# Giving the tile scheduler the order of every engine in an adaLN attention and MLP kernel, and splitting the modulation by PSUM bank

## The chip, the core and the metric

The kernel runs on one core of a Trainium2 chip. A core has TensorE (PE, with its weight loads shown as PEld), VectorE (DVE), ScalarE (ACT), GpSimd (POOL) and SyncE (SP, which here only issues DMAs). The metric is device time in microseconds (us) of one execution, the median over runs; the reading below is of one profiled execution.

## What is computed

One transformer layer on x of 2048 x 448 in bf16, with six modulation vectors made from c:

```
x = A_x
mod = (silu(c) @ w_mod).reshape(1, 6, 1, 448)
sa, ca, ga, sb, cb, gb = mod[:, 0], ..., mod[:, 5]
h = layernorm(x) * (1 + ca) + sa
x = x + ga * A_ref(h, A_wqkv, A_wo)
h = layernorm(x) * (1 + cb) + sb
x = x + gb * B_ref(h, B_w1, B_w2)
```

`A_ref` is attention with 16 heads of 28 columns, in which position s sees the 8 positions s, s-2, ..., s-14 (those below zero masked). `B_ref` is silu(h @ w1) @ w2 with 1792 hidden columns.

## The kernel before

Since attention reaches back in steps of 2, even and odd positions don't meet. They are two sequences ("parities") of 1024 positions, each of 8 tiles of 128 rows (u = 0 to 7 and 8 to 15) and of 9 attention blocks of up to 114 queries. A parity is worked in three groups, of 4, 3 and 2 blocks, so there are six groups, k = 0 to 5.

The steps of one group, with their lines:

- **LN1** (`stats` L174 to L177, normalize L185 or L449, `transposes` L195, `modulate` L204 on ACT and L206 on DVE): statistics of each tile on DVE (`BN_STATS`, `BN_AGGR`), 1/sqrt on POOL as an add and a pow, the normalised tile `xn` on DVE, four PE transposes for each tile into `ps_t`, and the modulation into `h1T`. For LN1 the four 112-row pieces k = 0 to 3 of `ps_t` are divided between DVE and ACT. `ps_t` takes two PSUM banks, k = 0, 1 in one and k = 2, 3 in the other.
- **project** (`qk_unit` L235, L237; `v_unit` L243, L245): q and k of a column range in four PSUM tiles of 8 matmuls each, cast to `qk` by ACT or DVE; v by blocks.
- **logits** (L265, `Exp` on ACT L267, mask on DVE L302), **attention times v** (`av` L330, reciprocal L332, scale L335; `tr` L343, L344), **output projection** with the residual (L350, L351).
- **LN2** as LN1, into `h2T`, all on DVE; **MLP** (f1: L395 and `Silu` on ACT L396; f2: L411, L415 and the store L416).

`late_mod` makes the other four modulation vectors: 32 matmuls L215 into `ps_m`, two gates of 4 matmuls L223 into `ps_g`, a copy of each gate on ACT (L224), and `wo` times its gate on DVE (L480). `gate_w2` multiplies `w2` by its gate on DVE, in two halves (L483). `check_sums` (L428 to L434) reduces the softmax sums to one flag, which every engine loads into a register; if the flag is positive the whole layer runs again in a safe form.

**What sets the order.** The Python code emits "units" in a written order; `weave` mixes a main list with a filler list by estimated costs. All of it stands under `with tc.manual_schedule():`, so each engine executes its instructions exactly in the order in which the code emits them. Within an engine an instruction that waits holds all those behind it. In that order the LN1 units of tiles 8 to 11 and 12 to 15 come at the end of the list of k = 0, woven with the output projections of that group, and the first projection of parity 1 comes in the filler of k = 1. `late_mod` is the last filler of the logits of k = 0; both halves of `gate_w2` are the last filler of the logits of k = 1. PSUM has two pools: `big`, three tiles of two banks (`ps_t`, `ps_qk`, `ps_v`, `ps_l`, `ps_h`), and `one`, two tiles of one bank (`ps_m`, `ps_g`, `ps_o`, `ps_ot`, `ps_wo`, `ps_y`, `ps_f`).

Of the kernel before, what the change touches and what calls it, by code (L numbers as in the profile page):

```python
# [23 lines left out]
HALO = 16  # L24
# [42 lines left out]
def layer(ctx, tc, io, safe):  # L67
# [13 lines left out]
    def ct(shape, name, dt=BF16):  # L81
        return const.tile(shape, dt, name=name)
# [32 lines left out]
    h1T = [ct([KP, KT, CW], f"h1T{p}") for p in range(2)]  # L115
# [51 lines left out]
    def stats(us):  # L167

        n = len(us)
        st = small.tile([128, 4, 6], F32, name="st")  # L170
        mv = small.tile([128, 4, 2], F32, name="mv", bufs=4)
        rs = small.tile([128, 4], F32, name="rs", bufs=4)
        for j, u in enumerate(us):
            V.bn_stats(out=st[:, j, :], in_=x_all[:, u, :])  # L174
            V.bn_aggr(out=mv[:, j, :], in_=st[:, j, :])  # L175
        G.tensor_tensor(out=rs[:, 0:n], in0=mv[:, 0:n, 1], in1=epsb[:, 0:n], op=ALU.add)  # L176
        G.tensor_tensor(out=rs[:, 0:n], in0=rs[:, 0:n], in1=negh[:, 0:n], op=ALU.pow)  # L177
        return mv, rs
# [10 lines left out]
    def transposes(ts, ps=None, j0=0):  # L189
        if ps is None:  # L190
            ps = big.tile([128, KT, 512], BF16, name="ps_t", tag="big")
        for j, t in enumerate(ts):
            c0 = 128 * (j0 + j)
            for k in range(KT):
                T.transpose(ps[:, k, c0:c0 + 128], t[:, KP * k:KP * k + 128], ident[:])  # L195
        return ps

    def modulate(ps, p0, n, dst, c0, which, act=()):

        for k in range(KT):  # L200
            o, i = dst[:, k, c0:c0 + n], ps[0:KP, k, p0:p0 + n]
            scale, shift = modc[:, 2 * which + 1, k:k + 1], modc[:, 2 * which, k:k + 1]
            if k in act:
                S.activation(out=o, in_=i, func=ACTF.Identity, scale=scale, bias=shift)  # L204
            else:
                V.tensor_scalar(out=o, in0=i, scalar1=scale, scalar2=shift, op0=ALU.mult, op1=ALU.add)  # L206
# [214 lines left out]
    def check_sums():  # L421

        n = 2 * NB * H
        ok = small.tile([128, n], F32, name="ok", bufs=1)
        cnt = small.tile([128, 1], F32, name="cnt", bufs=1)
        flag = small.tile([1, 1], I32, name="flag", bufs=1)
        rcf = rc[:].rearrange("p b h -> p (b h)")
        V.tensor_scalar(out=ok[:], in0=rcf, scalar1=LO, scalar2=None, op0=ALU.is_ge)  # L428
        V.scalar_tensor_tensor(out=ok[:], in0=rcf, scalar=HI, in1=ok[:], op0=ALU.is_le, op1=ALU.mult)
        V.tensor_reduce(out=cnt[:], in_=ok[:], axis=AX.X, op=ALU.add)  # L430
        ps = one.tile([128, 512], F32, name="ps_f", tag="one")
        T.matmul(ps[0:1, 0:1], lhsT=cnt[:], rhs=onesf[:], start=True, stop=True)
        V.tensor_scalar(out=flag[:], in0=ps[0:1, 0:1], scalar1=-1.0, scalar2=float(128 * n), op0=ALU.mult, op1=ALU.add)  # L433
        return nc.values_load(flag[:], min_val=0, max_val=128 * n)  # L434


    def ln1_units(us):
        held = {}

        def st():  # L440
            held["s"] = stats(us)

        def norm():
            mv, rs = held["s"]
            held["x"] = []
            for j, u in enumerate(us):
                t = xn[xc[0] % NX]
                xc[0] += 1
                V.tensor_scalar(out=t[:, 0:D], in0=x_all[:, u, :], scalar1=mv[:, j, 0:1], scalar2=rs[:, j:j + 1], op0=ALU.subtract, op1=ALU.mult)  # L449
                held["x"].append(t)  # L450

        def tr():
            ps = transposes(held["x"])
            modulate(ps, 0, 128 * len(us), h1T[us[0] // 8], HALO + 128 * (us[0] % 8), 0, act=(1, 3))
        return [(10.0, st), (10.0, norm), (900.0, tr)]

    st0 = stats([0, 1])
# [6 lines left out]
    ps0 = transposes(xa)  # L464
    xb = normalize([2, 3], *st1)
    mod_cols((0, 1), 0)
    ps1 = transposes(xb)
    modulate(ps0, 0, 256, h1T[0], HALO, 0, act=(1, 3))
    modulate(ps1, 0, 256, h1T[0], HALO + 256, 0, act=(1, 3))
    for kk in range(KT):  # L470
        V.tensor_copy(out=wp[:, kk, :, 0:DH], in_=wqkv[:, kk, 0:2 * D].rearrange("p (h d) -> p h d", d=DH))  # L471
    consts_late()
# [32 lines left out]
    if not safe:  # L505
        bad = check_sums()
# [6 lines left out]
@with_exitstack  # L513
def kernel(
    ctx: ExitStack,
    tc: tile.TileContext,
    A_x: bass.AP,
    A_wqkv: bass.AP,
    A_wo: bass.AP,
    B_x: bass.AP,  # L520
    B_w1: bass.AP,
    B_w2: bass.AP,
    c: bass.AP,
    w_mod: bass.AP,
    out: bass.AP,
):
    io = (A_x, A_wqkv, A_wo, B_w1, B_w2, c, w_mod, out)
    with ExitStack() as first:
        with tc.manual_schedule():
            bad = layer(first, tc, io, False)  # L530
    with tc.If(bad > 0):
        with ExitStack() as again:
            layer(again, tc, io, True)
# [30 lines left out]
```

## Time and profile before

| what | us |
|---|---|
| median of 3 runs (lowest, highest) | 246.09 (245.1, 246.82) |
| the profiled execution's own time | 246.31 |
| its span, first to last instruction | 244.5 |
| PE busy, and the five engines' next: DVE, ACT | 196.3, 125.3, 102.9 |
| PE busy in 57 to 81 us | 7.70 of 24.00 |
| PE busy in 99 to 219 us | 113.6 of 120.0 |

The profiled execution took 0.22 us more than the median. PE is the busiest engine, so the first thing to look for is where it has nothing to do. It stands idle in five places: while the first inputs load and LN1 of the first tiles is made (0 to 22 us), between 57 and 81 us, around 97 us, around 141 and 174 us, and briefly at 219 us.

### The profile page before, as it was taken

How to read it: one execution, taken by the hardware profiler on the slowest of the kernel's cores; microseconds unless marked ns; L12 is line 12 of the kernel's file. 1: busy time of each engine (PE TensorE's matmuls, PEld its weight loads, DVE VectorE, ACT ScalarE, POOL GpSimd, SP SyncE). 2: the span in 40 equal slices, each digit the busy share in tenths (PEclk: the TensorE clock that was granted, in tenths of full speed). 3: DMA queues.
4: the chain of work that ended last, by engine and by line, in shares of the span. 5: the costliest groups of instructions: out<-in, count | busy, mean ns of one | idle time of the engine just before them, and what ended most of it. 6: DMA issues, size and time to landing. Idle time of an engine off the chain costs nothing.

```text
span 244.5 us, 4117 instructions
## 1 busy us (share of the span) xinstructions
PE 196.3 (80%) x1739; PEld 118.7 (49%) x1739; DVE 125.3 (51%) x274; ACT 102.9 (42%) x133; POOL 16.8 (7%) x55
## 2 busy tenths in 40 slices
PE   0555979982522997899999959899599999989992
PEld 0413445661321544555665434786346555645760
DVE  4474406686683358557444164675357475554111
ACT  2032397701206157245543744624465373650330
POOL 3801000001030000010000100000100010010000
PEclk9998999998555699999999988999889999999999
DMA  6999995000000000000100001000000001000101
GB/s 166 249 227 230 235 213 165 4 3 0 0 0 0 3 0 1 3 0 20 39 0 3 0 5 35 20 3 0 3 19 21 0 0 40 19 0 23 38 5 44
DMA packets 9073, 11.22 MB, mean 46 GB/s; under 512 B 473, under 2 KB 8153, under 8 KB 9049
## 3 DMA queue, kind: packets, MB, share of 16 engines
q1 hardware_dynamic: 9040, 10.90, 18.7%
q8 instruction: 15, 0.25, 0.5%
q14 instruction: 10, 0.07, 0.1%
q10 hardware_dynamic: 8, 0.00, 0.0%
HBM read 9.06 MB, written 1.84 MB: 45 GB/s over the span
## 4 chain that ended last, share of the span: by engine, by line
PE 67%; DVE 15%; ACT 8%; DMA 3%; issue 3%; POOL 1%; SPq 0%; ACTq 0%
PE ps_h L395 18%; PE ps_y L411 17%; PE ps_qk L235 10%; PE ps_v L243 5%; PE ps_wo L350 5%; PE ps_t L195 4%; ACT p L267 4%; DMA wmod<-in_w_mod_dram 3%; PE ps_l L265 3%; DVE st L174 3%; DVE p L302 2%; DVE o L335 2%; PE ps_o L330 2%; ACT h1T L204 2%; ACT L267 2%
## 5 line engine op out<-in xcount | busy, mean ns | idle before, releaser
L395 PE MATMUL ps_h<-h2T,w 112*128 112x384 bf16 (+1 forms) x336 | 53.4, 308 | 0.0
L396 ACT ACTIVATE hid<-ps_h 128x768 bf16<-128x768 f32 (+1 forms) x42 | 31.0, 739 | 46.1 <-PE ps_h L395 46.0
L411 PE MATMUL ps_y<-w,hid 128*128 128x448 bf16 x224 | 48.5, 365 | 0.7 <-DVE flag L433 0.7
L267 ACT ACTIVATE p<-ps_l 128x912 bf16<-128x912 f32 (+1 forms) x36 | 33.2, 933 | 21.1 <-PE ps_l L265 21.1
L395 PEld LDWEIGHTS <-w 112*128 112x128 bf16 x336 | 32.3, 98 | 16.0
L302 DVE TENSOR_TENSOR p<-p,maskb 128x1824 bf16<-128x1824 bf16 (+1 forms) x18 | 19.9, 1107 | 37.5 <-ACT p L267 37.5
L235 PE MATMUL ps_qk<-h1T,wp 112*128 112x456 bf16 (+2 forms) x192 | 35.3, 334 | 4.2 <-DVE wp L471 2.8
L195 PE MATMUL ps_t<-ident,xn 128*128 128x128 bf16 x128 | 13.3, 276 | 26.4 <-DVE xn L449 14.7
L411 PEld LDWEIGHTS <-hid 128*128 128x128 bf16 x224 | 20.7, 100 | 20.4 <-issue 3.3
L235 PEld LDWEIGHTS <-wp 112*128 112x128 bf16 x192 | 18.6, 103 | 15.6 <-issue 5.2
L195 PEld LDWEIGHTS <-xn 128*128 128x128 bf16 x128 | 10.9, 125 | 29.9 <-DVE xn L449 16.7
L174 DVE BATCH_NORM_STATS2 st<-x_all 128x6 f32<-128x448 bf16 x32 | 19.2, 601 | 2.4 <-DMA x_all<-in_A_x_dram 2.4
L204 ACT ACTIVATE h1T<-ps_t,modc 112x512 bf16<-112x512 bf16 (+1 forms) x10 | 6.8, 691 | 31.3 <-DVE h1T L206 31.3
L415 DVE TENSOR_TENSOR ot<-ps_y,x_all 128x448 bf16<-128x448 f32 x16 | 9.9, 621 | 19.6 <-PE ps_y L411 19.6
L351 DVE TENSOR_TENSOR x_all<-ps_wo,x_all 128x448 bf16<-128x448 f32 x16 | 10.0, 623 | 14.7 <-PE ps_wo L350 14.7
L176 POOL TENSOR_TENSOR rs<-mv,epsb 128x2 f32<-128x2 f32 (+2 forms) x11 | 2.3, 206 | 199.8 <-DVE mv L175 199.8
L245 ACT CAST v<-ps_v 128x448 bf16<-128x448 f32 x18 | 8.8, 536 | 16.4 <-PE ps_v L243 16.3
L265 PE MATMUL ps_l<-qk 28*128 28x114 bf16 (+1 forms) x288 | 13.8, 221 | 2.3 <-ACT h1T L204 2.3
L350 PE MATMUL ps_wo<-wo,oT 112*128 112x448 bf16 x64 | 15.5, 367 | 0.2
L243 PE MATMUL ps_v<-wqkv,h1T 112*128 112x448 bf16 x72 | 15.1, 353 | 0.0
L265 PEld LDWEIGHTS <-qk 28*128 28x128 bf16 x288 | 8.0, 97 | 13.7 <-issue 13.3
L237 ACT CAST qk<-ps_qk 128x912 bf16<-128x912 f32 (+2 forms) x12 | 8.7, 728 | 12.7 <-PE ps_qk L235 12.6
(63 smaller groups left out, 154.8 us busy)
## 6 DMA issues: line engine op xcount, KB each, us to landing
w<-in_B_w_dram SPq DMA_DIRECT2D x2, 1568.0 KB, 23.0
out_dram<-ot SPq DMA_DIRECT2D x16, 112.0 KB, 1.7
wmod<-in_w_mod_dram SPq DMA_DIRECT2D x1, 1568.0 KB, 19.0
x_all<-in_A_x_dram SPq DMA_DIRECT2D x3, 448.0 KB, 17.9
wqkv<-in_A_wqkv_dram SPq DMA_DIRECT2D x3, 392.0 KB, 10.6
wmod<-in_w_mod_dram SPq DMA_DIRECT2D x1, 784.0 KB, 8.2
x_all<-in_A_x_dram SPq DMA_DIRECT2D x2, 224.0 KB, 2.9
wo<-in_A_wo_dram SPq DMA_DIRECT2D x1, 392.0 KB
```

The lines of the kernel that those rows point to most:

```text
L174: V.bn_stats(out=st[:, j, :], in_=x_all[:, u, :])
L195: T.transpose(ps[:, k, c0:c0 + 128], t[:, KP * k:KP * k + 128], ident[:])
L204: S.activation(out=o, in_=i, func=ACTF.Identity, scale=scale, bias=shift)
L235: T.matmul(ps[:, j, 0:n], lhsT=wp[:, k, 16 * typ + 4 * g:16 * typ + 4 * g + 4, :].rearrange("p h d -> p (h d)"), rhs=h1T[par][:, k, HALO + ...
L243: T.matmul(ps[:, j, 0:D], lhsT=h1T[par][:, k, BQ * b + 2:BQ * b + 130], rhs=wqkv[:, k, 2 * D:3 * D], start=(k == 0), stop=(k == KT - 1))
L265: T.matmul(ps[:, j, g * nq:(g + 1) * nq], lhsT=qk[par][r:r + DH, 4 + g, BQ * b + 2:BQ * b + 130], rhs=qk[par][r:r + DH, g, HALO + BQ * b:H ...
L267: S.activation(out=pbuf(par, b)[:, t, :, :, 0:nq], in_=ps[:, :, 0:4 * nq].rearrange("p j (g q) -> p j g q", q=nq), func=ACTF.Exp, scale=SCALE)
L302: V.tensor_tensor(out=p, in0=p, in1=maskb[:, 1 if b == 0 else 0, 0:nq].unsqueeze(1).to_broadcast([128, H, nq]), op=ALU.mult)
L350: T.matmul(ps[:, 0:D], lhsT=oT[par][:, kk, 128 * a:128 * a + 128], rhs=wo[:, kk, :], start=(kk == 0), stop=(kk == KT - 1))
L395: T.matmul(ps[:, j, 0:n], lhsT=w1[:, kk, 128 * f:128 * f + 128], rhs=h2T[k % 2][:, kk, 0:n], start=(kk == 0), stop=(kk == KT - 1))
L396: S.activation(out=hid[k % 2][:, 2 * i:2 * i + 2, 0:n], in_=ps[:, :, 0:n], func=ACTF.Silu)
L411: T.matmul(ps[:, 0:D], lhsT=hid[k % 2][:, f, 128 * j:128 * j + 128], rhs=w2[:, f, :], start=(f == 0), stop=(f == NF - 1))
```

## The change

The `with tc.manual_schedule():` goes. The same Python code emits the same instructions in the same order, but that order is now only a priority: the scheduler of the tile framework takes for each engine the next instruction that it believes ready, and so moves work forward past work that waits. In LN1 the division of `modulate` changes from k = 0, 2 on DVE and 1, 3 on ACT to k = 0, 1 on DVE and 2, 3 on ACT.

```
@@ in ln1_units, and twice in the start of layer @@
-            modulate(ps, 0, 128 * len(us), h1T[us[0] // 8], HALO + 128 * (us[0] % 8), 0, act=(1, 3))
+            modulate(ps, 0, 128 * len(us), h1T[us[0] // 8], HALO + 128 * (us[0] % 8), 0, act=(2, 3))
...
     with ExitStack() as first:
-        with tc.manual_schedule():
-            bad = layer(first, tc, io, False)
+        bad = layer(first, tc, io, False)
```

The list of instructions stays what it was; each engine's order differs as follows. Tile numbers in the names are two lower in the changed kernel (`p_110` and `p_108` are the same buffer).

**First place: DVE, at the end of the first projection.** `L174` and `L175` are LN1 statistics, `L449` the normalised tiles, `L237` casts of q and k, `L302` the masks of the logits. Before:

```order
L206 TENSOR_SCALAR h1T_92<-ps_t,modc 112x512 x2
L237 CAST qk<-ps_qk 128x2x456 x2
L302 TENSOR_TENSOR p_110<-p_110,maskb 128x16x114
L237 CAST qk<-ps_qk 128x2x342
L302 TENSOR_TENSOR p_111<-p_111,maskb 128x16x114
```

With the change:

```order
L237 CAST qk<-ps_qk 128x2x456
L174 BN_STATS st<-x_all 128x6 x2
L237 CAST qk<-ps_qk 128x2x456
L175 BN_AGGR mv<-st 128x2 x2
L174 BN_STATS st<-x_all 128x6 x2
L175 BN_AGGR mv<-st 128x2
L174 BN_STATS st<-x_all 128x6
L175 BN_AGGR mv<-st 128x2
L174 BN_STATS st<-x_all 128x6
L449 TENSOR_SCALAR xn_115<-x_all,mv,rs 128x448
L449 TENSOR_SCALAR xn_116<-x_all,mv,rs 128x448
```

The statistics of the eight tiles of parity 1, and six of their eight `xn`, now stand between the casts of the first projection and the first mask. Before, they stood behind the second output projection of k = 0. On PE the transposes of tiles 8 to 11 come with them, ahead of the first output projection. Also on PE, the 32 `ps_m` matmuls of `late_mod` and one of its two gates move from behind the seventh of the eight logits of k = 0 to behind the second.

**Second place: DVE, the two halves of `gate_w2`** (`L483`), before behind the masks of k = 1 and ahead of the scales `L335` of its first blocks:

```order
L302 TENSOR_TENSOR p_110<-p_110,maskb 128x16x114
L237 CAST qk<-ps_qk 128x2x456 x2
L302 TENSOR_TENSOR p_111<-p_111,maskb 128x16x114
L483 TENSOR_TENSOR w_77<-w_77,gbc 128x3136 x2
L332 RECIPROCAL rc<-ps_o 114x16
L335 TENSOR_TENSOR o_122<-ps_o,rc 114x448
```

The first half with the change, among the masks and scales of k = 0:

```order
L302 TENSOR_TENSOR p_110<-p_110,maskb 128x16x114
L483 TENSOR_TENSOR w_75<-w_75,gbc 128x3136
L302 TENSOR_TENSOR p_111<-p_111,maskb 128x16x114
L332 RECIPROCAL rc<-ps_o 114x16 x2
L335 TENSOR_TENSOR o_119<-ps_o,rc 114x448
```

The second half with the change, in the LN of k = 0 and 1 (`xn_115`, `xn_116` with `L449` are tiles 14 and 15 of LN1; `L185` are tiles 0 to 2 of LN2):

```order
L174 BN_STATS st<-x_all 128x6 x2
L175 BN_AGGR mv<-st 128x2
L449 TENSOR_SCALAR xn_115<-x_all,mv,rs 128x448
L175 BN_AGGR mv<-st 128x2
L449 TENSOR_SCALAR xn_116<-x_all,mv,rs 128x448
L302 TENSOR_TENSOR p_112<-p_112,maskb 128x16x114
L206 TENSOR_SCALAR h1T_91<-ps_t,modc 112x512 x2
L185 TENSOR_SCALAR xn_117<-x_all,mv,rs 128x448
L185 TENSOR_SCALAR xn_118<-x_all,mv,rs 128x448
L185 TENSOR_SCALAR xn_113<-x_all,mv,rs 128x448
L483 TENSOR_TENSOR w_75<-w_75,gbc 128x3136
L206 TENSOR_SCALAR h2T_94<-ps_t,modc 112x384 x4
```

One half now stands before the output projections of k = 0, the other behind the normalisation of LN2; none stands ahead of the scales of k = 1.

**Third place: DVE, LN2 in the later groups** (here that of k = 2; `L415` is the last step of the MLP). Before:

```order
L174 BN_STATS st<-x_all 128x6
L175 BN_AGGR mv<-st 128x2
L302 TENSOR_TENSOR p_114<-p_114,maskb 128x16x114
L185 TENSOR_SCALAR xn_119<-x_all,mv,rs 128x448
L185 TENSOR_SCALAR xn_120<-x_all,mv,rs 128x448
L206 TENSOR_SCALAR h2T_96<-ps_t,modc 112x256 x4
```

With the change:

```order
L174 BN_STATS st<-x_all 128x6
L175 BN_AGGR mv<-st 128x2
L185 TENSOR_SCALAR xn_117<-x_all,mv,rs 128x448
L185 TENSOR_SCALAR xn_118<-x_all,mv,rs 128x448
L206 TENSOR_SCALAR h2T_94<-ps_t,modc 112x256 x2
L302 TENSOR_TENSOR p_112<-p_112,maskb 128x16x114
L206 TENSOR_SCALAR h2T_94<-ps_t,modc 112x256 x2
```

The normalised tiles of LN2 now stand ahead of the first mask of the next logits. The same holds for k = 4. At the end, PE, DVE and ACT load the flag (L434) as their last instruction; before they did so in the middle, PE and DVE ahead of the last MLP steps.

## Rows read from the trace of the kernel before

**Rows 1.** The page: the span, and two groups of instructions (count | busy, mean ns | idle).

```profile
span 244.5 us, 4117 instructions
...
L174 DVE BATCH_NORM_STATS2 st<-x_all 128x6 f32<-128x448 bf16 x32 | 19.2, 601 | 2.4 <-DMA x_all<-in_A_x_dram 2.4
...
L351 DVE TENSOR_TENSOR x_all<-ps_wo,x_all 128x448 bf16<-128x448 f32 x16 | 10.0, 623 | 14.7 <-PE ps_wo L350 14.7
```

**Rows 2.** Two stretches by windows: each engine's busy us (instructions), granted clock as share.

```profile
57.00:81.00 24.00, 7.70 (x73) 5.84 (x74) 15.11 (x40) 5.57 (x7) 3.55 (x6) 0.55 0.00 0
...
83.00:85.00 2.00, 2.00 (x11) 0.92 (x9) 0.00 (x0) 0.92 (x1) 0.00 (x0) 0.88 0.00 0
```

**Rows 3.** The chain that ended last, 55 to 86 us: start, us, what.

```profile
55.78 0.77 PE ps_wo L350 x4
...
57.20 0.54 DVE st L174
...
60.49 1.02 POOL rs L177
...
66.38 0.54 DVE st L174
...
81.11 4.31 PE ps_qk L235 x16
```

**Rows 4.** Timeline of DVE, 28 to 97 us: start, us, line, operation [idle before <-releaser].

```profile
36.58 1.11 DVE L302 TENSOR_TENSOR p<-p,maskb 128x1824 bf16<-128x1824 bf16 x1 [6.62 <-ACT p L267]
...
63.91 0.54 DVE L206 TENSOR_SCALAR h1T<-ps_t,modc 112x512 bf16<-112x512 bf16 x1 [1.06 <-PE ps_t L195]
...
79.20 1.00 DVE L185 TENSOR_SCALAR xn<-x_all,mv,rs 128x448 bf16<-128x448 bf16 x3
...
93.73 3.49 DVE L483 TENSOR_TENSOR w<-w,gbc 128x3136 bf16<-128x3136 bf16 x2
```

**Rows 5.** The page's DMA issues: count, KB each, us from issue to landing.

```profile
wmod<-in_w_mod_dram SPq DMA_DIRECT2D x1, 1568.0 KB, 19.0
x_all<-in_A_x_dram SPq DMA_DIRECT2D x3, 448.0 KB, 17.9
wqkv<-in_A_wqkv_dram SPq DMA_DIRECT2D x3, 392.0 KB, 10.6
```

**Rows 6.** Timeline of SP's queue: when three of these loads were issued.

```profile
2.85 0.46 SPq L105 DMA_DIRECT2D wqkv<-in_A_wqkv_dram  x1
...
7.43 1.30 SPq L109 DMA_DIRECT2D wmod<-in_w_mod_dram  x1
8.78 5.90 SPq L98 DMA_DIRECT2D x_all<-in_A_x_dram  x2
```

**Rows 7.** Timeline of DVE, 13 to 22 us.

```profile
13.05 0.73 DVE L206 TENSOR_SCALAR h1T<-ps_t,modc 112x256 bf16<-112x256 bf16 x2 [0.70 <-ACT h1T L204]
...
20.84 1.31 DVE L449 TENSOR_SCALAR xn<-x_all,mv,rs 128x448 bf16<-128x448 bf16 x4 [1.41 <-POOL rs L177]
```

**Rows 8.** Timeline of PE, 35 to 99 us.

```profile
35.15 1.32 PE L235 MATMUL ps_qk<-h1T,wp 112*128 112x342 bf16 x8 [1.42 <-ACT p L267]
...
42.95 1.17 PE L215 MATMUL ps_m<-scT,wmod 112*128 112x1 bf16 x32
43.98 1.67 PE L223 MATMUL ps_g<-wmod,screp 112*128 112x448 bf16 x8
...
98.10 0.37 PE L343 MATMUL ps_ot<-ident,o 114*128 114x114 bf16 x4 [1.94 <-DVE o L335]
98.93 0.56 PE L330 MATMUL ps_o<-v,p 128*128 128x29 bf16 x16 [0.45 <-DVE o L335]
```

**Rows 9.** Timeline of PE, 143 to 220 us.

```profile
143.09 0.70 PE L195 MATMUL ps_t<-ident,xn 128*128 128x128 bf16 x8 [2.81 <-DVE xn L185]
...
175.57 1.45 PE L195 MATMUL ps_t<-ident,xn 128*128 128x128 bf16 x12 [2.60 <-DVE xn L185]
...
219.71 1.11 PE L411 MATMUL ps_y<-w,hid 128*128 128x448 bf16 x5 [0.74 <-DVE flag L433]
```

More of the change, by code (lines that the diff above doesn't have):

```diff
@@ L467, in layer @@
     ps1 = transposes(xb)
-    modulate(ps0, 0, 256, h1T[0], HALO, 0, act=(1, 3))
-    modulate(ps1, 0, 256, h1T[0], HALO + 256, 0, act=(1, 3))
+    modulate(ps0, 0, 256, h1T[0], HALO, 0, act=(2, 3))
+    modulate(ps1, 0, 256, h1T[0], HALO + 256, 0, act=(2, 3))
     for kk in range(KT):
```

## The prediction

> **What bounds the kernel now.** I read the span and the busy shares first, then the windows, then the chain that ended last, then the timelines of PE and DVE at each place where PE stands still, and the order of the changed program beside them. PE is busy 196 of the span's 244.5 us [rows 1], so what can be won is PE's idle time and its slow time. The windows show where that is. From 57 to 81 us PE works 7.70 of 24.00 us, DVE 15.11, and the granted clock averages 0.55, that is mostly the lower of TensorE's two levels (1.2 of 2.4 GHz) [rows 2]. The chain explains it [rows 3]: an output projection of PE ends at 56.55 (55.78 + 0.77), and the next projection starts at 81.11. In between the chain runs through LN1 statistics on DVE at 57.20, the POOL power at 60.49, statistics again at 66.38. These are for tiles 8 to 15, which depend on nothing but x. At 36.58 DVE had just been idle for 6.62 us [rows 4]. So the largest hole is a matter of order alone.
>
> The smaller holes are of the same kind. PE waits 1.42 us at 35.15, and 1.94 and 0.45 us at 98 us [rows 8] while DVE scales w2 for 3.49 us [rows 4]; and 2.81, 2.60 and 0.74 us for normalised tiles and the flag [rows 9].
>
> **The start (0 to 23 us): 0.** The wp copies now stand ahead of the first normalisations (first half of wqkv) and of the first modulations (second half). The second half was issued at 2.85 and the wqkv loads take 10.6 us to land (median): 13.45 [rows 5, 6]. Before, DVE at 13.05 had one modulation of four done and four copies ahead [rows 7]; now at 13.45 it has two copies and four modulations ahead. That is 0.4 late and one modulation more (0.37, half of the 0.73), two copies less: nothing. The next LN1 starts from DVE at about the same time, and PE needs its tiles, which came at 20.84 after 1.41 us of POOL [rows 7]. I take 0; bounds -0.4 and +1.5 (four modulations of 0.37 that nothing hides).
>
> **The logits of k = 0 (23 to 46 us): +0.8.** The 32 ps_m matmuls take 1.03 us (42.95 to 43.98) and half of the gates 0.83 (of 1.67) [rows 8]. Both move into the gap that begins at 33.73 (35.15 - 1.42). They end at 35.6, 0.44 later than PE went on before, and 1.86 us are gone from the place at 43: -1.4. Their load was issued at 7.43 and took 19.0 [rows 5, 6]: 26.4, well before 33.7.
>
> DVE pays for the statistics here. One with its aggregate is 0.75 to 0.8 us: four, with the first POOL step, go from 57.20 to 60.49 [rows 3]. Eight are some 6.2; six normalised tiles of 0.33 (1.31 / 4) 2.0; two POOL rounds of 1.41 [rows 7], some of the first filled, 2.0; two copies of ps_m 0.3. DVE is free from 29.96 (36.58 - 6.62), and squeezes two statistics (1.1) in before its last cast. So the first mask starts at 29.96 + 6.2 + 2.0 + 2.0 + 0.3 - 1.1 = 39.4 and not at 36.58. Behind it in DVE's queue stand wo times its gate and a cast of q or k, each about a mask's time (1.11 [rows 4]); the cast is out at about 42.3, and PE's fifth logits wait for it. PE gets there at about 40 (35.6 plus three units of 1.32 and two logits): 2.2 us of waiting. Together +0.8. Bounds: -1.4 (the wait does not bite) and +4 (the next cast is late as well).
>
> **The hole (46 to 81 us): -15.4, the 0.8 included.** On the way to the third output projection PE now does three things that lay in the hole: one more unit of 0.77 [rows 3] and 24 transposes (0.70 for 8 [rows 9], so 2.1). It has three qk units to do while DVE spends 1.75 on the first half of the w2 gate. So that projection ends at 56.55 + 0.8 + 0.8 + 2.1 = 60.2, less the short waits of PE that this work fills there; I take 59.2, between 57.7 and 61. From there the chain is DVE's: residual 0.62; two statistics 1.2 [rows 1]; their aggregates 0.2; two normalised tiles 0.66; the mask of block 4 1.11; two modulations of 0.54; three normalised tiles of LN2 1.00 [rows 4]; the last transposes 0.35. That is 6.2, with handoffs 6.5. Parity 1's projection starts at 65.7 and not at 81.11: -15.4. The clock: PE is again mostly idle for 6 us before it, and before the clock was back at 0.88 in 83 to 85, after the projection had begun [rows 2]; I leave that price in. If the clock stays up, 16 matmuls that took 4.31 [rows 3] take some 3.1: 1.2 less.
>
> **The gate of w2 (92 to 99 us): -2.4.** The waits of 1.94 and 0.45 [rows 8] go with the gate. Its second half (1.75) stands between LN2's normalisation and its modulation, beside two qk units of 4.31 on PE. Without that cover it costs 1.75. Bounds -2.8 and -0.6.
>
> **LN2 and the flag (130 to 220 us): -5.5.** With xn ahead of the mask, PE finds its tiles ready, and 2.81 + 2.60 us [rows 9] go; so does the 0.74 of the flag. What is late next is a PSUM tile of `big` that an exponential or the last modulation gives back, 0.3 us at each of two places: 6.15 - 0.6 = 5.5. Bounds -6.2 and -1. At the end DVE loads the flag beside the last store: 0, at most +0.7, the price of the wait at 219.
>
> **The bank split: 0.** At 13.05 DVE had waited 0.70 us for ACT [rows 7], though its piece (k = 2) and ACT's (k = 1) lie in different banks: the framework orders the readers of a tile, not of a bank. In the changed program ACT's first piece still waits for DVE's second. What goes is two handoffs, in places that wait for POOL or DVE anyway. The Trainium skill (PSUM — Partial Sum Buffer, Specifications) says that ScalarE and VectorE can read PSUM in parallel as long as their banks differ. By that rule the two would run together, and the sum would be 0.7 lower, the one modulation on the chain; the 0.70 speaks against its being used here.
>
> **Sum.** -15.4 - 2.4 - 5.5 = -23.3: from the profiled execution's 246.31 to 223.0 (a span of 221.2). That execution is 0.22 above the median, so I forecast a median of **222.8**.
>
> **Rivals.**
> - *DVE's queue takes part of it back* (231.9). At 98 us PE waited for scales [rows 8] whose inputs were there, behind a gate of 3.49 us [rows 4] that nobody needed yet. The change puts statistics, gates and LN2 tiles into the same queue earlier. If the next cast of k = 0 is late too (+3.2), the second w2 half delays LN2 (1.4 of the 2.4 lost) and the later holes open elsewhere (4.5 of 5.5 lost), the sum is -14.2. For it: DVE is the one engine whose order changes most. Against: from 99 us it is busy only half the time. The Trainium skill (TensorE: Matmul & The Clock Gate, Architectural detail: the array is 16× 32×32) says that DVE and ACT are strict FIFO; the trace agrees at 98 us.
> - *No change* (246): the hole is refilled. That needs 23 us of new waits; the loads of tiles 8 to 15, issued from 8.78 and 17.9 us to landing [rows 5, 6], would have to land past 50.
> - *Slower* (from 249): the same wait as a loss. The statistics stand at the head of DVE's queue, casts that PE needs behind them, so from about 31 us each us that those loads are late is a us of the whole. It decides at 23.3 + 2.5, when they land after about 57 us. Queue and order of the loads are as before, which speaks against it.
>
> **Chances.** The forecast 0.79, DVE's queue 0.15, no change 0.03, slower 0.03. The range takes the forecast with its bounds: down to 216 (the clock stays up, -1.2; the casts are not late, -2.2; the holes close wholly, -1.1; the projection ends at 57.7, -1.5; some of them together), up to 232, which holds the first rival. Faster by over 1% (2.5 us, about what a measurement can tell) 0.94, within 1% 0.03, slower 0.03.
>
> **What would show it.** Right: DVE statistics between 28 and 38 us; ps_m near 34 us; the first projection of parity 1 near 66 us; no idle time of PE over 1 us after 80 us but at the end; the last PE work 23 us earlier. Wrong in a step: PE waiting for a DVE cast at 40 us for more than 3 us, or not at all; transposes of tiles 8 to 15 still after 60 us; an idle PE before the LN2 transposes. The forecast fails if DVE's busy share between 28 and 66 us rises and PE's doesn't.

## The result, and the profile after

| kernel | median us (lowest to highest) | ratio to before, 95% interval |
|---|---|---|
| before | 246.45 (245.1 to 247.5) | 1 |
| changed | 217.65 (215.91 to 220.84) | 0.8811 [0.8733, 0.8888] |
| changed, run again (`after_again`) | 217.14 (215.45 to 220.28) | 0.8843 [0.8791, 0.8894] |

The change takes 28.8 us off; the forecast was 222.8, some 23 off, with a range of 216 to 232. The first profile of the changed kernel is of an execution of 220.84 us, 3.2 above the median; the second, `after_again`, is of one of 216.50. So the readings below are of the second, and the first is used, and named by its 220.84 us, where the two differ.

The page of `after_again`: span, busy time by engine, and the granted clock in 40 slices of 5.4 us.

```profile
span 214.8 us, 4124 instructions
...
PE 192.8 (90%) x1739; PEld 117.1 (55%) x1739; DVE 122.7 (57%) x274; ACT 102.0 (47%) x133; POOL 17.6 (8%) x55
...
PEclk9999999889975999999999999999999999999997
```

PE is busy for 90% of the span, where it was 80%. Before the end the clock dips in two places only, near 42 us and from 62 to 70 us.

The timeline of PE in `after_again` (start, us, line, what, [idle before <-releaser]): the rows that answer to [rows 3, 8, 9].

```profile
32.60 1.17 PE L215 MATMUL ps_m<-scT,wmod 112*128 112x1 bf16 x32
...
40.60 0.38 PE L265 MATMUL ps_l<-qk 28*128 28x114 bf16 x8 [1.75 <-DVE qk L237]
40.90 2.44 PE L243 MATMUL ps_v<-wqkv,h1T 112*128 112x448 bf16 x8
...
56.19 1.69 PE L350 MATMUL ps_wo<-wo,oT 112*128 112x448 bf16 x8
...
64.52 5.26 PE L235 MATMUL ps_qk<-h1T,wp 112*128 112x456 bf16 x15
...
121.44 0.62 PE L195 MATMUL ps_t<-ident,xn 128*128 128x128 bf16 x8
...
123.52 2.07 PE L411 MATMUL ps_y<-w,hid 128*128 128x448 bf16 x10
...
148.64 0.84 PE L195 MATMUL ps_t<-ident,xn 128*128 128x128 bf16 x12
```

The 32 `ps_m` matmuls came at 42.95 and come at 32.60. The new wait for a cast is there: 1.75 us. The third output projection of k = 0 ends at 57.9 (56.19 + 1.69), and parity 1's projection starts 6.6 us later (a single matmul of it stands earlier, at 63.29). The two LN2 transposes at 121.44 and 148.64 wait for nothing, and no PE row behind 62.89, up to the end, shows a wait.

Its timeline of DVE, for the same two places, answers to [rows 4]:

```profile
27.28 1.14 DVE L174 BATCH_NORM_STATS2 st<-x_all 128x6 f32<-128x448 bf16 x2
...
37.65 1.11 DVE L302 TENSOR_TENSOR p<-p,maskb 128x1824 bf16<-128x1824 bf16 x1
38.67 1.09 DVE L480 TENSOR_TENSOR wo<-wo,gbc 112x1792 bf16<-112x1792 bf16 x1
39.68 0.87 DVE L237 CAST qk<-ps_qk 128x684 bf16<-128x684 f32 x1
```

The statistics of tiles 8 to 15 begin at 27.28, the first mask stands behind them (37.65), and the cast that PE waits for is the third from there (39.68).

One row of PE's timeline from each stretch, before and after, makes the ledger. The shift grows by what each stretch gives.

| PE starts | before | changed | shift | what the stretch gave | forecast |
|---|---|---|---|---|---|
| first logits of k = 0 | 31.78 | 30.72 | -1.06 | start -1.1 | 0 |
| first projection of parity 1 | 80.90 | 64.52 | -16.38 | hole, with the wait at 40 us: -15.3 | -15.4 |
| third f1 unit of group 0 | 99.54 | 80.57 | -18.97 | gate of w2: -2.6 | -2.4 |
| last f2 units | 234.22 | 204.36 | -29.86 | LN2 and flag: -10.9 | -5.5 |

At the third f1 unit the two orders have not done quite the same work. At the first logits of the next group they have (108.61 before, 89.84 changed): there the gate's stretch has given 2.4. It is a net: the first projection of parity 1 takes 0.7 us longer than before (5.26 us for 15 matmuls, 4.51 for 16), and the rest of the stretch gives 3.1.

### The profile page after: what moved, and what is told of

The parts are those of the page before. It is cut to its first block, busy times and chain, and to the rows that moved or that the text cites. A ratio compares the mean times of both kernels' runs of the same rounds, so it can differ in the third digit from the quotient of the medians.

```text
span 219.0 us, 4124 instructions
## 1 busy us (share of the span) xinstructions
PE 194.5 (89%) x1739; PEld 118.0 (54%) x1739; DVE 122.7 (56%) x274; ACT 102.2 (47%) x133; POOL 17.3 (8%) x55
## 4 chain that ended last, share of the span: by engine, by line
PE 75%; DMA 9%; DVE 7%; SPq 4%; POOL 2%; issue 1%
PE ps_h L395 22%; PE ps_y L411 20%; PE ps_qk L235 9%; DMA x_all<-in_A_x_dram 9%; PE ps_v L243 6%; PE ps_wo L350 5%; PE ps_l L265 4%; PE ps_o L330 3%; PE ps_t L195 3%; DVE st L174 2%; PE ps_ot L343 2%; POOL rs L177 1%; SPq L108 1%; DVE xn L449 1%; SPq L98 1%; DVE qk L237 1%
## 5 line engine op out<-in xcount | busy, mean ns | idle before, releaser
L411 PE MATMUL ps_y<-w,hid 128*128 128x448 bf16 x224 | 46.3, 353 | 0.0
L267 ACT ACTIVATE p<-ps_l 128x912 bf16<-128x912 f32 (+1 forms) x36 | 33.1, 934 | 15.5 <-PE ps_l L265 15.4
L235 PE MATMUL ps_qk<-h1T,wp 112*128 112x456 bf16 (+2 forms) x192 | 36.6, 340 | 1.1 <-DVE h1T L206 0.7
L411 PEld LDWEIGHTS <-hid 128*128 128x128 bf16 x224 | 20.1, 98 | 18.2
L302 DVE TENSOR_TENSOR p<-p,maskb 128x1824 bf16<-128x1824 bf16 (+1 forms) x18 | 19.8, 1103 | 13.6 <-ACT p L267 13.6
L235 PEld LDWEIGHTS <-wp 112*128 112x128 bf16 x192 | 19.2, 105 | 12.8 <-issue 6.1
L174 DVE BATCH_NORM_STATS2 st<-x_all 128x6 f32<-128x448 bf16 x32 | 19.2, 614 | 3.8 <-DMA x_all<-in_A_x_dram 3.4
L415 DVE TENSOR_TENSOR ot<-ps_y,x_all 128x448 bf16<-128x448 f32 x16 | 9.9, 622 | 19.5 <-PE ps_y L411 19.5
L243 PE MATMUL ps_v<-wqkv,h1T 112*128 112x448 bf16 x72 | 17.7, 389 | 0.0
L176 POOL TENSOR_TENSOR rs<-mv,epsb 128x2 f32<-128x2 f32 (+2 forms) x11 | 3.2, 293 | 173.6 <-DVE mv L175 173.6
L206 DVE TENSOR_SCALAR h2T<-ps_t,modc 112x384 bf16<-112x384 bf16 (+1 forms) x24 | 9.4, 448 | 11.8 <-PE ps_t L195 11.8
L195 PE MATMUL ps_t<-ident,xn 128*128 128x128 bf16 x128 | 12.2, 251 | 3.7 <-DVE xn L185 2.5
L350 PE MATMUL ps_wo<-wo,oT 112*128 112x448 bf16 x64 | 14.6, 353 | 0.0
L237 ACT CAST qk<-ps_qk 128x912 bf16<-128x912 f32 (+2 forms) x12 | 8.8, 731 | 10.5 <-PE ps_qk L235 10.5
```

Source lines behind the costliest of these rows:

```text
L235: T.matmul(ps[:, j, 0:n], lhsT=wp[:, k, 16 * typ + 4 * g:16 * typ + 4 * g + 4, :].rearrange("p h d -> p (h d)"), rhs=h1T[par][:, k, HALO + ...
L237: (S.copy if on_act else V.tensor_copy)(out=dst, in_=ps[:, :, 0:n])
L243: T.matmul(ps[:, j, 0:D], lhsT=h1T[par][:, k, BQ * b + 2:BQ * b + 130], rhs=wqkv[:, k, 2 * D:3 * D], start=(k == 0), stop=(k == KT - 1))
L267: S.activation(out=pbuf(par, b)[:, t, :, :, 0:nq], in_=ps[:, :, 0:4 * nq].rearrange("p j (g q) -> p j g q", q=nq), func=ACTF.Exp, scale=SCALE)
L302: V.tensor_tensor(out=p, in0=p, in1=maskb[:, 1 if b == 0 else 0, 0:nq].unsqueeze(1).to_broadcast([128, H, nq]), op=ALU.mult)
L350: T.matmul(ps[:, 0:D], lhsT=oT[par][:, kk, 128 * a:128 * a + 128], rhs=wo[:, kk, :], start=(kk == 0), stop=(kk == KT - 1))
```

## The experiments

The theory after the result: the order does what the prediction says, and each PE wait that went took with it a second price, matmuls behind it at the lower clock (1.2 GHz, a granted clock of 0.50). Its rival: the waits alone count. All ratios are to the kernel before.

**The changed kernel once more** (no edit).

> The changed kernel once more, so that the next three can be set against it on one chip. Both theories: 0.881 of the kernel before, 217 to 218 us; in the trace a TensorE wait of about 2.8 us near 40 us with the granted clock at 0.50 for some 10 us behind it, if that was no accident of one execution. If the lower clock there is missing in this execution and the time is 4 to 5 us shorter, it comes and goes.

0.8843 [0.8791, 0.8894]. The wait is there in both executions, and of different length. Granted clock by windows (each row: the stretch, its length, the busy us of PE, PEld, DVE, ACT and POOL with their instructions, the granted clock, the DMA share, GB/s), first the execution of 220.84 us, where the wait was 2.83 us:

```profile
42.00:44.00 2.00, 1.86 (x12) 0.89 (x12) 1.88 (x3) 0.93 (x1) 0.00 (x0) 0.50 0.04 9
...
48.00:50.00 2.00, 2.00 (x14) 0.65 (x12) 0.78 (x1) 1.36 (x2) 0.00 (x0) 0.50 0.00 0
```

and then that of 216.50, with 1.75 us:

```profile
42.00:44.00 2.00, 2.00 (x13) 0.76 (x12) 0.34 (x1) 0.62 (x2) 0.00 (x0) 0.50 0.00 0
44.00:46.00 2.00, 2.00 (x15) 0.75 (x14) 0.78 (x1) 1.81 (x4) 0.00 (x0) 0.73 0.00 0
46.00:48.00 2.00, 2.00 (x38) 1.53 (x37) 1.13 (x2) 2.00 (x4) 0.00 (x0) 1.00 0.00 0
```

In the first the clock stays at 0.50 from 42 to beyond 50 us, in the second to 45 only. From the first logits to the first 226-column unit the two take 19.24 us (31.18 to 50.42) and 16.02 (30.72 to 46.74): 1.1 us of the difference is the wait, 2.1 the clock behind it. The price comes and goes, as the expectation had it. The longer wait has its own cause: in the execution of 220.84 us the load of x is late, and DVE's first statistics of tiles 8 to 15 wait for it, where those at 27.28 above waited for nothing:

```profile
28.83 1.15 DVE L174 BATCH_NORM_STATS2 st<-x_all 128x6 f32<-128x448 bf16 x2 [1.00 <-DMA x_all<-in_A_x_dram]
```

Counted from the first logits, the cast behind them is 1.1 us later (41.22 and 39.68), and PE waits as much longer for it.

**The wait at 40 us taken away.**

```
-        units = [(8 * n / 2.4, lambda i=i: qk_unit(par, cols, i, i % 2 == 0)) for i in (2, 0, 3, 1)]
+        units = [(8 * n / 2.4, lambda i=i: qk_unit(par, cols, i, k == 1 or i % 2 == 0)) for i in (2, 0, 3, 1)]
```

> The changed kernel; of the second projection of parity 0 all four casts are on ScalarE, where two were on VectorE behind the statistics and the first mask. It takes away what TensorE waits for at 42.13 us. Theory (a wait of that length also brings the matmuls behind it to the lower clock): the 2.83 us of waiting go down to under 1, and the granted clock stays at 1.00 from 42 to 52 us, which is worth another 4 to 5 us of matmuls; 4.5 to 7.5 us less than the changed kernel, 210 to 213 us. Rival 1 (only the wait counts, the lower clock comes from something else): 1.8 to 2.8 us less, 215 to 216 us, the clock still at 0.50 behind 42 us. Rival 2 (ScalarE now is late with the exponentials, and the VectorE chain at 62 to 68 us ends when it did): no change.

214.25 us, 0.8746 [0.8696, 0.8797]: 2.9 us less than the changed kernel beside it. PE and its clock there:

```profile
39.82 0.37 PE L265 MATMUL ps_l<-qk 28*128 28x114 bf16 x8
40.12 1.69 PE L243 MATMUL ps_v<-wqkv,h1T 112*128 112x448 bf16 x8
```

```profile
42.00:44.00 2.00, 2.00 (x22) 0.83 (x16) 0.32 (x1) 2.00 (x5) 0.00 (x0) 1.00 0.00 0
```

The wait is gone and the clock stays up; eight `ps_v` matmuls take 1.69 us, not 2.44 or 3.17. By its time alone this run would also fit the first rival (1.8 to 2.8 us less); the clock row speaks for the theory. Between the rows named above this kernel takes 12.63 us (31.75 to 44.38), 3.4 less than `after_again`: 1.75 of waiting and 1.6 of clock. The 4.5 to 7.5 us expected were taken from the execution of 220.84 us, where both were larger (19.24 - 12.63 = 6.6: 2.83 and 3.8).

**One half of the change each.** `split_alone` edits the kernel before in the three LN1 calls, `sched_alone` the changed kernel back:

```
split_alone   -act=(1, 3)  +act=(2, 3)
sched_alone   -act=(2, 3)  +act=(1, 3)
```

> The kernel before with the order still fixed by hand; only the modulation of LN1 is split into pieces 0 and 1 on VectorE and 2 and 3 on ScalarE. Theory: nothing, 0.998 to 1.002 of before, because the two engines still take turns on one ps_t. Rival, by the PSUM page of the Trainium skill (both engines at once in different banks): 0.7 us for each of the modulations on the chain, 0.7 to 3 us in all, ratio 0.988 to 0.997, with the ScalarE pieces beside the VectorE pieces in the trace.

> The changed kernel with the modulation split as before (pieces 0 and 2 on VectorE, 1 and 3 on ScalarE): the scheduler's order alone. Theory: the same as the changed kernel within 1 us, ratio 0.877 to 0.885. Rival, if the bank split carries part of the gain: 0.7 to 3 us slower than the changed kernel, ratio 0.884 to 0.894.

`sched_alone`: 0.8853 [0.8799, 0.8906], the changed kernel's time without the split. So the order carries the gain. Its profile has the wait for the cast too, of 1.73 us, as long as in `after_again`; but behind it the clock is at 0.50 from 44 to 50 us and not to 45 only:

```profile
46.00:48.00 2.00, 2.00 (x13) 0.72 (x12) 1.11 (x1) 1.70 (x3) 0.00 (x0) 0.50 0.00 0
```

`split_alone`: 0.9862 [0.9797, 0.9927], 3.4 us less than before, where I expected nothing. Its DVE at the start, its ACT, and its PE:

```profile
11.73 1.37 DVE L206 TENSOR_SCALAR h1T<-ps_t,modc 112x256 bf16<-112x256 bf16 x4
13.01 1.29 DVE L471 COPY wp<-wqkv 112x896 bf16<-112x896 bf16 x4
```

```profile
12.56 1.93 ACT L204 ACTIVATE h1T<-ps_t,modc 112x256 bf16<-112x256 bf16 x4 [9.07 <-DVE h1T L206]
```

```profile
13.46 3.22 PE L235 MATMUL ps_qk<-h1T,wp 112*128 112x456 bf16 x8 [1.16 <-DVE wp L471]
```

DVE's four pieces now run without a break and the `wp` copies start at 13.01, not 14.88: the first projection starts 1.9 us earlier (13.46 for 15.32), of which 0.2 is `ps_m` starting earlier (9.88 for 10.10). At the LN2 transposes of group 0 it is 2.2 (77.49 for 79.65). By these rows that is what the split is worth in the old order. In this execution the clock also stayed up behind the waits at 141 and 172 us, though nothing fills them (1.00 in 143 to 147 us, where before has 0.50 from 145), which the experiments on LN2 take up. Within a tile the two engines still take turns: ACT begins at 12.56, after DVE's second piece. The Trainium skill (PSUM — Partial Sum Buffer, Specifications (TRN2)) lets the two read different banks at once; no run here shows them do it in one tile. In the scheduler's order the copies stand ahead of the modulations anyway, and the 1.9 us are gone as a separate gain.

**LN2 ahead of the mask, by hand.**

```
     def ln2_stats(k):
         ln2[k] = stats(us_of(k))
+        if k >= 1:
+            ln2[k] = normalize(us_of(k), *ln2[k])
...
-            ln2[k] = normalize(us, *ln2[k])
+            if k < 1:
+                ln2[k] = normalize(us, *ln2[k])
```

> The kernel before, its order fixed by hand; only the normalisation of LN2 for the groups 1 to 4 is emitted right behind its statistics, ahead of the first mask of the next logits. The flag's wait stays. Forecast of the prediction's term without the flag, waits alone: 2.81 + 2.60 less 0.6 = 4.8 us less, ratio 0.980. Theory (waits and the lower clock behind them): another 1.6 us at each of the two places, 8 to 9 us less, ratio 0.963 to 0.968, and the granted clock at 1.00 where it was 0.50 from 145 to 148 and from 176 to 179 us.

0.981 [0.9745, 0.9874], 4.7 us less (3.1 to 6.3): the waits' price. Yet the profile has both parts:

```profile
140.90 0.62 PE L195 MATMUL ps_t<-ident,xn 128*128 128x128 bf16 x8
...
212.20 0.19 PE L435 MATMUL ps_f<-onesf,cnt 128*1 128x1 f32 x2 [1.38 <-DVE cnt L433]
```

Both waits are gone, the clock is 1.00 behind both places, and a new wait of 1.38 us stands before the flag. And the lower clock stands at another place: 0.53 in 99 to 101 us, behind the 1.94 us that PE waits for scales, where before has 1.00 behind the same wait. This run alone does not separate the theories.

**Useless work in the waits.** In the kernel before, PE transposes the identity 42 times into the PSUM tile that it is about to fill, first (`fill_the_wait`) with the counts {2: 42, 4: 42} (group: transposes), then (`fill_both_waits`) with {2: 42, 3: 42}:

```
-            ps = transposes(ln2[k])
+            ps = big.tile([128, KT, 512], BF16, name="ps_t", tag="big")
+            for _ in range(FILL.get(k, 0)):
+                T.transpose(ps[:, 0, 0:128], ident[:], ident[:])
+            transposes(ln2[k], ps)
```

> The kernel before with its order and its late normalisations; ahead of the LN2 transposes of the groups 2 and 4 TensorE does 42 transposes of the identity matrix into the same PSUM tile, whose result is overwritten: some 2.3 us of useless work in each of the two waits (2.81 and 2.60 us). The waits for the normalised tiles stay as they are. Theory (idle time before it is what lowers the clock): the matmuls behind the two places run at 1.00, some 1.6 us less at each, 2.5 to 3.5 us less in all, ratio 0.986 to 0.990, although work was added. Rival (the lower clock there is not due to the idle time): no change, or slower by what of the 84 transposes sticks out.

1.0078 [1.0043, 1.0113], slower by 1.9 us: the second lot stood at the wrong group, at 197 us, where nothing waits, and cost its 2.5 us whole. With the second lot at group 3:

> As fill_the_wait, with the 42 useless transposes now ahead of the LN2 transposes of the groups 2 and 3, the two places where TensorE waits 2.81 and 2.60 us (in fill_the_wait the second lot stood at group 4, where nothing waits, and cost 2.5 us). Theory (the idle time is what brings the clock down behind it): the granted clock is 1.00 behind both places in every execution, and the time is that of those executions of before in which the clock stayed up: 243 to 245 us, ratio 0.988 to 0.997. Rival (the clock falls there whatever TensorE does in the wait): ratio 1.000 to 1.005 and 0.50 behind the places.

0.9942 [0.9902, 0.9983]: 1.4 us faster (0.4 to 2.4) with 84 matmuls more. Its profile:

```profile
139.97 2.52 PE L386 MATMUL ps_t<-ident 128*128 128x128 bf16 x42
...
144.95 2.07 PE L415 MATMUL ps_y<-w,hid 128*128 128x448 bf16 x10
...
171.05 2.52 PE L386 MATMUL ps_t<-ident 128*128 128x128 bf16 x42
```

The same ten `ps_y` matmuls took 3.50 us at 145.38 in the kernel before, at this granted clock:

```profile
145.00:147.00 2.00, 2.00 (x13) 0.93 (x12) 1.21 (x3) 1.00 (x2) 0.00 (x0) 0.50 0.16 57
```

That the time falls although work was added is what shows that PE's idle time carries a clock's price here; the one profile alone would not, since in `split_alone` both waits stood empty and the clock stayed up as well. So the price is not paid every time. In `fill_the_wait` too the second wait, 2.60 us, was left empty, and the clock behind it stayed up:

```profile
174.93 1.01 PE L196 MATMUL ps_t<-ident,xn 128*128 128x128 bf16 x12 [2.60 <-DVE xn L186]
```

```profile
176.00:178.00 2.00, 2.00 (x24) 0.99 (x21) 2.00 (x5) 1.42 (x2) 0.00 (x0) 1.00 0.00 0
```

**The hole alone, by hand.** Statistics of tiles 8 to 15 and four normalised tiles go ahead of the logits of k = 0:

```
+    la, lb = ln1_units([8, 9, 10, 11]), ln1_units([12, 13, 14, 15])
+    run([la[0], lb[0], la[1]])
...
-            fill = project(1) + [(2000.0, late_mod)]
+            fill = project(1) + [la[2], (2000.0, late_mod)]
...
-            main = project(2) + ln1_units([8, 9, 10, 11]) + ln1_units([12, 13, 14, 15])
+            main = [lb[1], lb[2]] + project(2)
```

> The kernel before, its order fixed by hand; only LN1 of tiles 8 to 15 is emitted earlier: both statistics and the first four normalised tiles ahead of the logits of group 0, the first transposes among them, the rest ahead of the third projection. Gates, ps_m and LN2 as before. The prediction's term for the hole without the clock: 15 to 17 us less, ratio 0.93 to 0.94. Theory (the early statistics make TensorE wait for a cast near 40 us, and that wait brings the lower clock as in the changed kernel): 11 to 14 us less, ratio 0.943 to 0.955, with 0.50 of clock behind 40 us.

0.9815 [0.9749, 0.9881], only 4.6 us less: both expectations missed. PE waits elsewhere, and at half the clock:

```profile
50.96 1.89 PE L195 MATMUL ps_t<-ident,xn 128*128 128x128 bf16 x16 [1.94 <-DVE xn L449]
...
55.70 0.61 PE L330 MATMUL ps_o<-v,p 128*128 128x29 bf16 x16 [2.05 <-DVE o L335]
```

```profile
46.00:48.00 2.00, 1.69 (x8) 0.52 (x10) 0.26 (x3) 1.85 (x3) 0.00 (x0) 0.50 0.00 0
...
62.00:64.00 2.00, 2.00 (x12) 1.30 (x11) 0.40 (x1) 0.54 (x1) 0.00 (x0) 0.50 0.00 0
```

The second four tiles stand in DVE's queue behind `wo` times its gate and a mask, the modulations behind them hold the scales, and the clock is low from 45 to 65 us. The second output projection ends 8 us later than before (64.7 for 56.5), the third 1 us (66.4 for 65.4). And one fall of the clock is not explained by waiting:

```profile
44.00:44.50 0.50, 0.50 (x13) 0.41 (x11) 0.50 (x2) 0.00 (x0) 0.00 (x0) 0.92 0.00 0
44.50:45.00 0.50, 0.50 (x3) 0.22 (x2) 0.23 (x1) 0.24 (x1) 0.00 (x0) 0.50 0.00 0
```

The longest that PE had waited in the nine us before is 0.41 us, at 41.92, ahead of 16 transposes; then come 8 logits and 32 matmuls of one column. What brought the clock down there is open.

An order moved in one block moves the hole; the scheduler's order puts the same pieces singly between others. That this is the reason is argued; which of its other moves carries the rest of the 15 us was not separated.

**The gate alone, by hand.** The first half goes behind `late_mod`, the second between normalisation and modulation of LN2 of group 0:

```
-            fill = project(1) + [(2000.0, late_mod)]
+            fill = project(1) + [(2000.0, late_mod), (10.0, lambda: gate_w2(0, 7))]
...
-            fill = ln2_units(0) + project(3) + [(10.0, lambda: gate_w2(0, 7)), (10.0, lambda: gate_w2(7, 14))]
+            u = ln2_units(0)
+            fill = u[:1] + [(10.0, lambda: gate_w2(7, 14))] + u[1:] + project(3)
```

> The kernel before, its order fixed by hand; only the two halves of the w2 gate are emitted earlier, the first behind the gates of group 0, the second between normalisation and modulation of LN2 of group 0. The prediction's term: the waits of 1.94 and 0.45 us go, 2.4 us less, ratio 0.988 to 0.992. In the rows of before the clock is 1.00 behind these two waits, so both theories give the same. Rival (VectorE is the next to be late there): under 1 us.

1.0177 [1.0117, 1.0237]: 4.4 us slower. The waits at 98 us go, and this one comes, on DVE and then on PE:

```profile
47.80 1.79 DVE L483 TENSOR_TENSOR w<-w,gbc 128x3136 bf16<-128x3136 bf16 x1
```

```profile
50.47 0.37 PE L343 MATMUL ps_ot<-ident,o 114*128 114x114 bf16 x4 [2.37 <-DVE o L335]
```

It was 0.67 us there before. The half stands ahead of the first scale of k = 0, and the clock falls to 0.50 by 54 us behind it. At 143 us the net is +0.4; beyond that the profile shows a longer stretch at 0.50 behind the second LN2 wait (176 to 182 us; before, 0.74 in 178 to 180). The profiled execution is the fastest of the four, only 1.3 us above that of before; what makes the other three slower (248.9 to 250.2) no trace shows. In the changed program the same half runs at 47.20, between two masks, where DVE had just been idle for 0.87 us. The gate's gain seems to hang on that place.

**Tiles 8 to 15 loaded last**, an edit of the changed kernel:

```
-    xload(8, 12)
-    xload(12, 16)
     nc.sync.dma_start(out=w1[:], in_=rows(B_w1))
     nc.sync.dma_start(out=w2[:], in_=B_w2.rearrange("(f p) d -> p f d", p=128))
+    xload(8, 12)
+    xload(12, 16)
```

> The changed kernel; x of tiles 8 to 15 is loaded behind w1 and w2 instead of ahead of them. It undoes what lets the hole close: statistics that depend on nothing but an early load. In the program the masks of group 0 now stand ahead of most of these statistics. Theory (the gain at 57 to 81 us comes from statistics made before 38 us): the wait for a cast at 40 us goes, 1.8 to 2.8 us, but statistics, normalised tiles and modulations come back into the stretch before the first projection of parity 1, 5 to 8 us of VectorE work: 3 to 8 us more than the changed kernel, 220 to 226 us. Rival (these statistics find room beside the logits of group 0 anyway, and their place ahead of the masks only cost): 0 to 3 us less than the changed kernel.

217.77 us, 0.8845 [0.8796, 0.8895]: no difference; the theory is refuted, and the rival holds only at its edge. PE there:

```profile
41.67 0.92 PE L243 MATMUL ps_v<-wqkv,h1T 112*128 112x448 bf16 x4 [0.91 <-DVE qk L237]
...
59.94 1.38 PE L195 MATMUL ps_t<-ident,xn 128*128 128x128 bf16 x16 [3.75 <-DVE xn L449]
...
64.90 4.79 PE L235 MATMUL ps_qk<-h1T,wp 112*128 112x456 bf16 x16
```

Both things happen: the wait at 40 us shrinks and the clock stays at 1.00 up to 60 us, and 3.75 us of waiting come back ahead of the projection, which starts at 64.90 for 64.52. They cancel. So the hole does not hang on statistics before 38 us: six of the eight now run from 39 to 46 us, beside the masks, and that is early enough.

**Two versions beyond**, edits of `cast_on_act`:

```
cast_and_xn    -NV, NP, NX = 10, 5, 6   +NV, NP, NX = 10, 5, 8
casts_and_xn   as cast_and_xn, and   -k == 1 or   +k in (1, 2) or
```

> cast_on_act with eight buffers for normalised tiles instead of six, so that the last two of LN1 are made near 39 us and not at the end of the VectorE chain near 58 us. If that chain sets the start of parity 1's projection there, 0.7 us less than cast_on_act (two tiles of 0.36 us), 213 to 214 us. Rival (the transposes and modulations that now come earlier take the same time from that chain): no difference.

> cast_and_xn with the casts of the third projection on ScalarE as well. It takes 1.24 us of casts (two of 0.62) off VectorE at 51 to 54 us; but the scheduler moves the second half of the w2 gate (1.78 us) ahead of the third block's scales there. By these rows 0.5 us more than cast_and_xn, 213.5 to 214.5 us. Rival (that half stood behind the normalisation of LN2 at 61 us, on the same chain): up to 1.2 us less, 212 to 213 us.

213.9 us, 0.8693 [0.8651, 0.8735], and 213.38 us, 0.8688 [0.8644, 0.8733]. Both beat the changed kernel by 3 to 4 us; the steps between them and `cast_on_act` are too small for these intervals. From the third output projection to parity 1's projection it is still 6.7 us in `cast_and_xn` (54.4 to 61.1), as in `cast_on_act`; what PE waits for there is now a mask:

```profile
58.30 0.53 PE L330 MATMUL ps_o<-v,p 128*128 128x29 bf16 x13 [1.84 <-DVE p L302]
```

## Why the prediction was right, and which step was mis-sized

- **Start, 0.** -1.1 in `after_again`, -0.6 in the execution of 220.84 us, both below the bound of -0.4. In the new order DVE waits first for wqkv, until 10.91 and 12.08 us, so the start depends on that load: in `cast_on_act`, where the copies begin at 12.15, the first logits come at 31.75, as before.
- **Logits of k = 0, +0.8, and the hole, -15.4 in all.** Right in mechanism and place: the wait was forecast at 2.2 us and is 1.75 and 2.83; the third output projection at 59.2 ended at 57.9 in an execution that began 1.1 earlier; the chain of 6.5 us took 6.6. That the sum agrees to 0.1 is luck in part. The logits gave +1.9 (16.02 us for 14.11), since the clock behind the wait, 1.6 us, is in no term; the rest of the way to the projection gave about as much more (-17.2, not -16.2). One of the prediction's own signs of a wrong step also showed: transposes of tiles 14 and 15 still come at 60.09. Its own chain, with their normalised tiles behind 59.2, implies as much, so the sign was badly chosen. In the execution of 220.84 us the stretch gave 12 (68.78 for 80.90), because of the longer wait and the clock behind it. The prediction's lower bound for the logits, -1.4 without the wait, is what `cast_on_act` shows: its 12.63 us took 14.11 before (31.78 to 45.89).
- **Gate of w2, -2.4.** -2.6, or -2.4 at equal work, as a net of more than one effect (see the ledger). By hand, in other places, the same move cost time.
- **LN2 and the flag, -5.5.** This is the step that was mis-sized: -10.9. The three waits [rows 9] went whole, 6.15; nothing was late next, so the 0.6 kept back, for which no row gave a size, did not come. 3.2 us are the clock, in [rows 9] itself: 8 and 12 transposes took 0.70 and 1.45 us where they now take 0.62 and 0.84, and the `ps_y` rows behind them the rest (1.43 and 0.74 us; two logits 0.19 each). The last 1.5 are what is left, smaller waits that I had not listed, the largest 0.63 us at 155.83 for DVE's residual add (L415). The prediction priced a wait by its idle time alone, though its own [rows 2] showed the lower level behind the large hole. As a median this clock price is below 3.2, since it is not paid in every execution: filling the two waits gave 1.4 us.
- **Bank split, 0.** Right for the changed kernel. For the old order the reason was wrong: its two handoffs did not all lie in places that wait anyway, and are worth some 1.7 us at the start (the 1.9 less the 0.2 of `ps_m`).
- **Rivals.** DVE's queue takes back the wait at 40 us, which the forecast has in it, and nothing later: after 63 us PE shows no wait. The mechanism that the prediction named under *Slower* is there, small: in the execution of 220.84 us x came late, DVE's statistics waited 1.00 us for it at 28.83, and PE's wait at 40 us is 1.1 us longer. Behind w1 and w2 the loads cost nothing in the time.

## What to carry to other kernels

Price a wait of the bottleneck engine by its idle time and by what its next matmuls take in the rows: at LN2 a wait of under 3 us cost up to 1.7 us more, and behind the one of 2.83 us the clock was halved for over 8 us, which cost another 3.8. What the scheduler gained here by many single moves was not had by moving one block by hand; the statistics and the gate, moved so, stood ahead of what PE waited for. After a reordering, look for the first new wait and ask whether another engine is idle there: two casts moved to ACT gave 2.9 us more.

## What the hardware showed that I had not expected

The clock behind a wait of one length is not the same from one execution to the next: 0.50 for over 8 us behind 2.83 us, for some 3 behind 1.75, for over 6 behind 1.73 in `sched_alone`, not at all behind 2.60 in `fill_the_wait` nor behind 2.81 and 2.60 in `split_alone`. The Trainium skill (TensorE: Matmul & The Clock Gate, HAM oscillation — how this bites in real kernels) says that waits between bursts of matmuls bring the array back to half its clock, so that each burst starts slow. The traces agree, with the addition that here it happens in some executions and not in others. The fall at 44 us in `ln1_by_hand`, with no wait of more than 0.41 us ahead of it, is not covered by it.

In `after_again` the POOL add of LN2 of group 0 takes six times what the other adds take, while DVE runs a mask from 60.32 to 61.42 us:

```profile
31.38 0.20 POOL L176 TENSOR_TENSOR rs<-mv,epsb 128x4 f32<-128x4 f32 x1 [12.18 <-DVE mv L175]
...
60.20 1.27 POOL L176 TENSOR_TENSOR rs<-mv,epsb 128x3 f32<-128x3 f32 x1 [23.20 <-DVE mv L175]
```

The price is small: the normalised tile at 62.43 needs it, but DVE is busy until 62.33 anyway. In `cast_on_act` and `sched_alone` the same add takes 1.27 us again, beside a mask (at 58.49 and 63.41). The Trainium skill (SBUF — State Buffer, SBUF: two separate sides) says that DVE and GpSimd share a pair of ports, which one instruction holds to its end. The 1.27 us fit that: the mask's 1.10 and the add's own 0.20. But the add's record begins 0.12 us ahead of the mask's, so which of the two held the ports is not shown. In `loads_last` the same add, beside normalised tiles, took 0.26.
